# Expert weights' low parts on VectorE, and the float64 decode started with the first expert

## The chip, the cores and the metric

The kernel runs on one core of one Trainium2 chip. The metric is the device time of one execution in microseconds (us); 0.3% of it is about what a measurement of this kernel can tell from no change. The engines are TensorE (PE, with its weight loads as PEld), VectorE (DVE), ScalarE (ACT), GpSimd (POOL) and SyncE (SP, whose queue SPq issues nearly all DMAs). Each engine works its own instructions strictly in the order of its queue.

## What is computed

Three layers in a row on 3072 tokens of 320 numbers (4 sequences of 768, 8 heads of 40):

```
attention:  state = state * w_t - (state @ a_t) b_t + v_t k_t ;  y_t = r_t @ state      (768 steps)
experts:    e = argmax(x @ w_gate);  out = gate * (relu(x @ w1[e]) @ w2[e])              (8 experts, 320 -> 1024 -> 320)
last layer: h = x @ w_in;  g = max(h, 0) + alpha * min(h, 0);  out = g @ w_out           (320 -> 2048 -> 320)
```

`w_in` and `w_out` arrive as float64; everything else is float32.

## The kernel before

**Stages.** The attention runs from the start of the span to about 500 us, the experts from 500 to about 760 us, the last layer from there to the end. The change lies in the expert stage alone.

**One expert.** Tokens have been sorted by expert into the DRAM tensor `xs_d` (room for 448 each). `load_x` brings them in, TensorE transposes them (`tr_ps`, L270), ACT and DVE split them into a rounded part `xthi` (L271, L273) and a rest `xtlo` (L274, L276). For each of eight blocks `f` of 128 hidden units TensorE makes `ph` (8 matmuls of 448 columns, `hidden`), ACT writes `hh` = relu(ph) rounded (L1111), DVE writes its rest `hl` (L1114, two pieces, one of them stored behind `hh`), and one block later TensorE adds that block into the four sums `po` (11 matmuls of 320 columns, `layer2`). So a block's `hh` and `hl` have about one block of TensorE's time to be ready. Sums go out through `ye` (L1172 to L1175) to `ys_d`. The first expert is cut in two: 256 tokens first, the other 192 in a second group; `between(f)` is called in the second group only.

**Preparing weights.** `prep_expert(e + 1, engine)`, called in block 1 of expert e, loads six pieces of float32 weights into `raw` (three buffers, L1047 and L1063); ACT rounds each piece into `we` (L1048, L1064), and the engine that was handed over writes the low part, `raw` minus the rounded part, into `we` as well (L1050, L1052, L1065). A buffer of `raw` comes free when the low part is written. Expert 0 is prepared during the attention, on DVE; experts 1 to 7 are prepared on GpSimd.

**The decode.** `decode` turns `w_in` and `w_out` from float64 into float32 in DRAM: 20 chunks, each a load `r64` (512 KB, L1026; two buffers), three bit operations on DVE (L214, L215, L216 into `dec`), a test on ACT (L1030, L1033) and a store (L1034). The profile prints `r64` as `r`. The decoded weights are read back late, as `raw<-w_in`, for the last layer, and split there on GpSimd (before and after alike).

**Order.** A scheduler with a model of its own time lays down the order of each engine's queue when the program is built. A call such as `decode` only sets where in the program the work enters that model; rows can move by several blocks.

Of the kernel before, what the change touches and what calls it, by code (L numbers as in the profile page):

```python
# [236 lines left out]
def whole(gen):  # L237
    for _ in gen:
        pass
# [749 lines left out]
class Moe:  # L989
# [142 lines left out]
    def run(self, ctx, to_flag):  # L1132
        nc, k, tc = self.nc, self.k, self.tc
        for i in (1, 2):
            self.wp.append(ctx.enter_context(tc.tile_pool(name=f"fm_w{i}", bufs=1, reuse_waits="tile")))
        cp = ctx.enter_context(tc.tile_pool(name="fm_c", bufs=1, reuse_waits="tile"))
        sp = self.sp = ctx.enter_context(tc.tile_pool(name="fm_s", bufs=2, reuse_waits="tile"))
        pg = self.pg = ctx.enter_context(tc.tile_pool(name="fm_pg", bufs=2, space=PSUM, reuse_waits="tile"))
        self.ptr = ctx.enter_context(tc.tile_pool(name="fm_pt", bufs=2, space=PSUM, reuse_waits="tile"))
        pb = ctx.enter_context(tc.tile_pool(name="fm_pb", bufs=1, space=PSUM, reuse_waits="tile"))  # L1140
        pa = ctx.enter_context(tc.tile_pool(name="fm_pa", bufs=1, space=PSUM, reuse_waits="tile"))
        sums = lambda: [p.tile([P, DM], F32, name=f"po{t}") for t, p in enumerate((pa, pa, pb, pb))]
        r6 = ExitStack()
        self.r6 = r6.enter_context(tc.tile_pool(name="fm_r6", bufs=1, reuse_waits="tile"))
        self.small = cp.tile([P, 20], F32, name="small")
        self.n_small = 0
        load = self.load_x(0, EARLY)
        nxt = win = prep = w_in = w_out = None
        for e in range(E):
            w1s, w2s = self.wts[e]  # L1150
            po = sums()
            ye = sp.tile([P, 4, DM], F32, name="ye", tag="orow", bufs=1)
            ys = self.rt.ys_d[e * CAP:(e + 1) * CAP, :]

            def group(xt, t0, t1, x0, tiles, ts=None, between=None):

                ts = ts or range(t0, t1)
                n = min(t1 * P, CAP) - t0 * P
                prev = None
                for f in range(NF1):  # L1160
                    hh, hl = tiles(f)
                    self.hidden(w1s, f, xt, x0, x0 + n, hh, hl)
                    if prev is not None:
                        self.layer2(po, *prev, w2s, f - 1, NF1, True, ts, t0)
                    prev = hh, hl
                    if between:
                        between(f)
                self.layer2(po, *prev, w2s, NF1 - 1, NF1, True, ts, t0)

            def to_sbuf(t):  # L1170
                if t == 3:
                    nc.scalar.copy(ye[:HT, t, :], po[t][HT:])  # L1172
                    nc.vector.tensor_tensor(ye[:HT, t, :], po[t][:HT], ye[:HT, t, :], op=ALU.add)
                else:
                    (nc.vector.tensor_copy if t % 2 else nc.scalar.copy)(ye[:, t, :], po[t])  # L1175

            def between(f):
                nonlocal nxt, win, prep, w_in, w_out
                if e == E - 2 and f == 4:
                    win = self.whole("win")  # L1180
                    prep = self.prep_in(win, w_in, nc.gpsimd)
                if e == E - 2 and f >= 4:
                    for _ in range(2):
                        next(prep, None)
                if e == E - 1:
                    with tc.issue_after(self.hh_i.ins):
                        next(prep, None)
                if f == 1 and e + 1 < E:
                    with tc.issue_after(self.rt.last.ins), tc.issue_after(self.x_dma.ins):
                        whole(self.prep_expert(e + 1, nc.gpsimd))  # L1190
                if (e, f) == (E - 1, 4):
                    assert self.n_small == 20
                    to_flag(self.psum_t(P)[:1], self.small)
                if (e, f) == (1, 0):
                    with tc.issue_after(self.hh_i.ins), tc.issue_after(self.hl_i.ins):
                        w_in, w_out = self.decode(self.w_in, "w_in"), self.decode(self.w_out, "w_out")
                if f == 4 and e + 1 < E:
                    nxt = self.load_x(e + 1)()

            ring = lambda f: [sp.tile([P, 4 * P], F32R, name=n, tag=n) for n in ("hh", "hl")]  # L1200
            if e == 0:
                group(self.xt0, 0, EARLY, 0, lambda f: [self.ap.tile([P, EARLY * P], F32R, name=n, bufs=2) for n in ("ehh", "ehl")])
                xt = load()
                group(xt, EARLY, 4, 0, ring, between=between)
            elif e == E - 1:

                hs = [[hp.tile([P, 2 * P], F32R, name=f"{n}{f}") for n in ("hh", "hl")] for f in range(NF1)]
                group(xt, 0, 2, 0, lambda f: hs[f], (0,), between)
                to_sbuf(0)
                nc.sync.dma_start(ys[:P, :], ye[:, 0])  # L1210
                with tc.issue_after(self.last.ins):
                    for f in range(NF1):
                        self.layer2(po, *hs[f], w2s, f, NF1, True, (1,))
                    group(xt, 2, 4, 2 * P, ring)
            else:
                group(xt, 0, 4, 0, ring, between=between)
            for t in range(1 if e == E - 1 else 0, 4):
                to_sbuf(t)
            for rows, to in self.rows(ye, ys, 1 if e == E - 1 else 0):
                nc.sync.dma_start(to, rows)  # L1220
            if e == E - 2:
                r6.close()
                hp = ctx.enter_context(tc.tile_pool(name="fm_h", bufs=1, reuse_waits="tile"))
                wout = self.whole("wout")
                prep = self.prep_out(wout, w_out, nc.gpsimd)
                win = win.rearrange("p (c f) -> p c f", c=5)
                wout = wout.rearrange("p (s f d) -> p s f d", s=2, d=DM)
            xt = nxt

        al = cp.tile([P, NF2], F32, name="al")  # L1230
        nc.sync.dma_start(al, self.alpha.rearrange("(f p) -> p f", p=P))
        BT = 512
        xt = self.load_x2(0, (E - 1) * CAP + P)
        for i in range(N // BT):
            po = sums()
            prev = None
            for f in range(NF2):
                ph = pg.tile([P, BT], F32, name="ph")
                gemm_k(nc, ph, win, f * P, (f + 1) * P, xt, 0, BT)
                g = sp.tile([P, BT], F32, name="g")  # L1240
                nc.vector.tensor_scalar(g, ph, 0.0, al[:, f:f + 1], op0=ALU.min, op1=ALU.mult)  # L1241
                nc.vector.scalar_tensor_tensor(g, ph, 0.0, g, op0=ALU.max, op1=ALU.add)  # L1242
                hh = sp.tile([P, BT], F32R, name="gh", tag="hh")
                hl = sp.tile([P, BT], F32R, name="gl", tag="hl")
                lo = split(nc, hh, hl, g, nc.gpsimd)
                if prev is not None:
                    self.layer2(po, *prev, wout, f - 1, NF2, False)
                prev = (hh, hl)
                if f == 8 and i + 1 < N // BT:
                    with tc.issue_after(lo.ins):  # L1250
                        nxt = self.load_x2(i + 1, E * CAP)
            ot = sp.tile([P, 4, DM], F32, name="ot", tag="orow", bufs=1)
            for j, (b, t) in enumerate(self.tokens(i)):
                self.layer2(po, *prev, wout, NF2 - 1, NF2, False, (j,))
                gate = self.rt.gate[:, b, t:t + 1]
                if j % 2:
                    nc.vector.tensor_scalar(ot[:, j, :], po[j], gate, None, op0=ALU.mult)
                else:
                    nc.scalar.activation(ot[:, j, :], po[j], AF.Copy, scale=gate)
                if j >= 2:  # L1260
                    at = (b * (S // P) + t - 1) * P
                    nc.sync.dma_start(self.out[at:at + 2 * P, :].rearrange("(t p) d -> p t d", p=P), ot[:, j - 2::2])
            xt = nxt
# [91 lines left out]
```

## Time and profile before

| | us |
|---|---|
| median of 3 runs (lowest, highest) | 1121.48 (1121.19, 1124.84) |
| the profiled execution's own time | 1123.27 |
| its span, first to last instruction | 1121.4 |
| TensorE busy in the span | 1016.5 (91%) |
| DVE busy | 671.7 (60%) |
| ACT busy | 587.3 (52%) |
| GpSimd busy | 546.9 (49%) |
| mean granted TensorE clock | 0.941 |

The span is all but 1.9 us of the profiled execution. Shares are means over stages with different limits; the expert stage is read below in stretches that end where expert 0, 1, 2, 3 and 4 write their last output piece (the end of L1173 at 547.7, 583.6, 612.7, 642.9 and 674.8 us).

### The profile page before, as it was taken

How to read it: one execution, taken by the hardware profiler on the slowest of the kernel's cores; microseconds unless marked ns; L12 is line 12 of the kernel's file. 1: busy time of each engine (PE TensorE's matmuls, PEld its weight loads, DVE VectorE, ACT ScalarE, POOL GpSimd, SP SyncE). 2: the span in 40 equal slices, each digit the busy share in tenths (PEclk: the TensorE clock that was granted, in tenths of full speed). 3: DMA queues.
4: the chain of work that ended last, by engine and by line, in shares of the span. 5: the costliest groups of instructions: out<-in, count | busy, mean ns of one | idle time of the engine just before them, and what ended most of it. 6: DMA issues, size and time to landing. Idle time of an engine off the chain costs nothing.

```text
span 1121.4 us, 24836 instructions
## 1 busy us (share of the span) xinstructions
PE 1016.5 (91%) x9597; PEld 895.2 (80%) x9597; DVE 671.7 (60%) x1451; ACT 587.3 (52%) x1481; POOL 546.9 (49%) x496
## 2 busy tenths in 40 slices
PE   3669899899799999889799989999999999999996
PEld 2558778777677877678698879988888898988996
DVE  8885968968589584543588863334444434444532
ACT  3647887788788886764576644432222222221211
POOL 7755664674656423225555444553434343534332
PEclk8669998999899996999899999999999999999998
DMA  4632322332332122416798954420000000000000
GB/s 120 195 118 59 96 62 77 89 92 78 81 79 69 53 64 64 136 37 201 231 296 271 315 152 144 139 83 15 24 24 24 25 25 24 24 25 24 24 1 27
DMA packets 98081, 103.36 MB, mean 92 GB/s; under 512 B 58404, under 2 KB 78884, under 8 KB 97956
## 3 DMA queue, kind: packets, MB, share of 16 engines
q1 hardware_dynamic: 95652, 93.83, 28.2%
q0 software_dynamic: 2304, 7.87, 2.2%
q8 instruction: 78, 1.28, 0.5%
q14 instruction: 47, 0.39, 0.1%
HBM read 79.39 MB, written 22.28 MB: 91 GB/s over the span
## 4 chain that ended last, share of the span: by engine, by line
PE 52%; DVE 6%; DMA 6%; ACT 4%; issue 2%; SPq 0%; POOL 0%; DVEq 0%; ACTq 0%; POOLq 0%
PE ph L243 22%; PE po L243 20%; DMA raw<-in_moe_w_dram 2%; PE sa L660 2%; PE tr_ps L270 1%; PE pp L620 1%; PE yc L676 1%; DMA r<-in_moe_w_in_dram 1%; DVE dec L215 1%; DMA r<-in_moe_w_out_dram 1%; DVE dec L214 1%; PE rvp L631 1%; PE rp L648 1%; PE xp L243 1%; PE lp L488 1%
## 5 line engine op out<-in xcount | busy, mean ns | idle before, releaser
L234 POOL TENSOR_TENSOR gl<-g,gh 128x512 fp32r<-128x512 f32 x96 | 123.7, 1291 | 214.6 <-ACT gh L233 123.2
L233 ACT ACTIVATE gh<-g 128x512 fp32r<-128x512 f32 x96 | 60.8, 633 | 252.0 <-DVE g L1242 172.0
L1241 DVE TENSOR_SCALAR g<-ph,al 128x512 f32<-128x512 f32 x96 | 72.2, 752 | 160.0 <-POOL gl L234 77.7
L243 PE MATMUL ph<-x2thi,win 128*128 128x512 f32 x480 | 159.5, 397 | 0.0
L243 PE MATMUL po<-wout,gh 128*128 128x320 f32 x768 | 139.0, 309 | 0.0
L243 PEld LDWEIGHTS po<-wout,gh 128*128 128x128 f32 x768 | 122.0, 188 | 5.6
L243 PE MATMUL ph<-x2tlo,win 128*128 128x512 f32 x288 | 114.3, 397 | 0.0
L243 PE MATMUL po<-we,hh 128*128 128x320 f32 x480 | 91.2, 317 | 14.1 <-DVE hh L1114 10.0
L243 PEld LDWEIGHTS ph<-x2thi,win 128*128 128x128 f32 x480 | 88.6, 188 | 14.9
L243 PE MATMUL ph<-xthi,we 128*128 128x448 f32 (+2 forms) x360 | 98.0, 344 | 1.0 <-ACT xthi L273 1.0
L243 PEld LDWEIGHTS po<-we,hh 128*128 128x128 f32 x480 | 74.3, 182 | 18.9 <-DVE hh L1114 10.9
L243 PE MATMUL po<-wout,gl 128*128 128x320 f32 x384 | 82.9, 311 | 0.0
L469 POOL TENSOR_TENSOR abd<-ra,q 40x512 f32<-40x512 f32 x44 | 64.4, 1463 | 25.4 <-PE ap L512 13.0
L243 PE MATMUL ph<-xtlo,we 128*128 128x448 f32 (+2 forms) x216 | 74.1, 344 | 0.3 <-DVE xtlo L276 0.3
L488 PE MATMUL lp<-kb,abd 128*128 128x128 f32 x352 | 58.7, 317 | 15.5 <-POOL abd L469 10.0
L634 POOL TENSOR_SCALAR_AFFINE_SELECT va<-vg 64x512 f32<-64x512 f32 x48 | 33.0, 688 | 77.0 <-ACT vg L633 47.5
L243 PEld LDWEIGHTS ph<-xthi,we 128*128 128x128 f32 x360 | 66.6, 195 | 4.4 <-ACT xthi L273 1.1
L1242 DVE SCALAR_TENSOR_TENSOR g<-ph,g 128x512 f32<-128x512 f32 x96 | 66.3, 691 | 3.1
L1111 ACT ACTIVATE hh<-ph 128x448 fp32r<-128x448 f32 (+2 forms) x72 | 34.2, 477 | 61.5 <-PE ph L243 47.1
L243 PEld LDWEIGHTS po<-wout,gl 128*128 128x128 f32 x384 | 64.0, 188 | 3.0
L488 PEld LDWEIGHTS lp<-kb,abd 128*128 128x128 f32 x352 | 50.9, 222 | 19.3 <-POOL abd L469 11.0
L1050 POOL TENSOR_TENSOR we<-raw,we 128x1024 fp32r<-128x1024 f32 x14 | 34.1, 2452 | 65.3 <-ACT we L1048 63.3
(217 smaller groups left out, 2388.3 us busy)
## 6 DMA issues: line engine op xcount, KB each, us to landing
raw<-in_moe_w_dram SPq DMA_DIRECT2D x16, 512.0 KB
rv<-in_rvP_dram SPq DMA_DIRECT2D x48, 160.0 KB
raw<-in_moe_w_dram SPq DMA_DIRECT2D x16, 480.0 KB
kb<-in_kbP_dram SPq DMA_DIRECT2D x44, 160.0 KB
r<-in_moe_w_in_dram SPq DMA_DIRECT2D x10, 512.0 KB
r<-in_moe_w_out_dram SPq DMA_DIRECT2D x10, 512.0 KB
xs_d<-tt SPq DMA_DIRECT2D x8, 560.0 KB
raw<-in_moe_w_dram SPq DMA_DIRECT2D x16, 256.0 KB
```

The source lines that it names most:

```text
L214: nc.vector.tensor_scalar(t, up, 0x07FFFFFF, 3, op0=ALU.bitwise_and, op1=ALU.logical_shift_left)
L233: nc.scalar.activation(hi, src, AF.Copy)
L234: return lo_eng.tensor_tensor(lo, src, f32(hi), op=ALU.subtract)
L243: return nc.tensor.matmul(out, lhsT=lhsT, rhs=rhs, start=start, stop=stop)
L469: nc.gpsimd.tensor_tensor(abd[r, :, q * C:(q + 1) * C], ra[r], qc[r, :, :C], op=ALU.mult)
L488: nc.tensor.matmul(lp[:, i], lhsT=abd[:, i, c2, :], rhs=kb[:, i, c2, :], start=True, stop=True)
L634: nc.gpsimd.affine_select(x.va[:C].rearrange("p a b c -> p (a b) c")[:, :, D:], x.vg[:C].rearrange("p a b c -> p (a b) c")[:, :, D:], patt ...
L660: nc.tensor.matmul(sa[q * 64:q * 64 + 64, i], lhsT=x.pw[:, i, q * C:(q + 1) * C], rhs=x.vg[:, i, q, :], start=True, stop=True)
L1050: eng.tensor_tensor(wt[:, 3 + c, cs], raw, f32(wt[:, c, cs]), op=ALU.subtract)
L1111: self.hh_i = nc.scalar.activation(hh[:, :n], ph[:, :n], AF.Relu)
L1241: nc.vector.tensor_scalar(g, ph, 0.0, al[:, f:f + 1], op0=ALU.min, op1=ALU.mult)
L1242: nc.vector.scalar_tensor_tensor(g, ph, 0.0, g, op0=ALU.max, op1=ALU.add)
```

## The change

Two calls in `between` differ. The low parts of experts 1 to 7 are handed to DVE, and `decode` is called in block 0 of expert 0's second group instead of block 0 of expert 1.

```diff
                 if f == 1 and e + 1 < E:
                     with tc.issue_after(self.rt.last.ins), tc.issue_after(self.x_dma.ins):
-                        whole(self.prep_expert(e + 1, nc.gpsimd))
+                        whole(self.prep_expert(e + 1, nc.vector))
...
-                if (e, f) == (1, 0):
+                if (e, f) == (0, 0):
                     with tc.issue_after(self.hh_i.ins), tc.issue_after(self.hl_i.ins):
                         w_in, w_out = self.decode(self.w_in, "w_in"), self.decode(self.w_out, "w_out")
```

What stands in the queues changes with it, from expert 0's second group into expert 5; the attention and the last layer keep their order. DVE, expert 0's second group, from block 1 to block 2 (`hh`/`hl` of one block, then of the next). Before:

```order
L1114 SCALAR_TENSOR_TENSOR hh_7297<-ph_7299,hh_7297 128x64
L1114 SCALAR_TENSOR_TENSOR hl_7298<-ph_7299,hh_7297 128x128
L1114 SCALAR_TENSOR_TENSOR hh_7342<-ph_7344,hh_7342 128x64
L1114 SCALAR_TENSOR_TENSOR hl_7343<-ph_7344,hh_7342 128x128
L1114 SCALAR_TENSOR_TENSOR hh_7361<-ph_7363,hh_7361 128x64
```

The same place now (`we1` is expert 1's weights):

```order
L1114 SCALAR_TENSOR_TENSOR hl_7500<-ph_7501,hh_7499 128x128
L215 SCALAR_TENSOR_TENSOR dec_7300<-r64_7298,dec_7300 128x512
L274 TENSOR_TENSOR xtlo_7605<-tr_ps_7606,xthi_7604 128x448
L215 SCALAR_TENSOR_TENSOR dec_7310<-r64_7308,dec_7310 128x512
L274 TENSOR_TENSOR xtlo_7605<-tr_ps_7613,xthi_7604 128x448
L216 SCALAR_TENSOR_TENSOR dec_7300<-r64_7298,dec_7300 128x512
L1065 TENSOR_TENSOR we1_7518<-raw_7532,we1_7518 128x960
L216 SCALAR_TENSOR_TENSOR dec_7310<-r64_7308,dec_7310 128x512
L1065 TENSOR_TENSOR we1_7518<-raw_7536,we1_7518 128x960
L1114 SCALAR_TENSOR_TENSOR hh_7544<-ph_7546,hh_7544 128x64
```

Where two blocks followed each other directly, eight operations now stand between them: four of the decode, two of expert 1's tokens, two low parts.

SP's queue, as expert 1's loads begin. Before:

```order
L1078 DMA xe_7104<-xs_d_79 64x320
L1047 DMA raw_7317<-in_moe_w1_dram 128x1024
L1047 DMA raw_7321<-in_moe_w1_dram 128x1024
L1047 DMA raw_7325<-in_moe_w1_dram 64x1024 x2
L1026 DMA r64_7516<-in_moe2_w_in_dram 128x1024
L1026 DMA r64_7526<-in_moe2_w_in_dram 128x1024
```

Now:

```order
L1078 DMA xe_7104<-xs_d_79 64x320
L1026 DMA r64_7298<-in_moe2_w_in_dram 128x1024
L1026 DMA r64_7308<-in_moe2_w_in_dram 128x1024
L1047 DMA raw_7519<-in_moe_w1_dram 128x1024
L1047 DMA raw_7523<-in_moe_w1_dram 128x1024
L1047 DMA raw_7527<-in_moe_w1_dram 64x1024 x2
```

The first two loads of the decode, which stood behind the first three pieces of expert 1's weights, now stand ahead of them.

DVE at the start of expert 4 (its blocks 0 and 1), before:

```order
L214 TENSOR_SCALAR dec_7699<-r64_7697 128x512
L1114 SCALAR_TENSOR_TENSOR hh_8515<-ph_8517,hh_8515 128x64
L1114 SCALAR_TENSOR_TENSOR hl_8516<-ph_8517,hh_8515 128x384
L215 SCALAR_TENSOR_TENSOR dec_7699<-r64_7697,dec_7699 128x512
L1114 SCALAR_TENSOR_TENSOR hh_8566<-ph_8568,hh_8566 128x64
L1114 SCALAR_TENSOR_TENSOR hl_8567<-ph_8568,hh_8566 128x384
L216 SCALAR_TENSOR_TENSOR dec_7699<-r64_7697,dec_7699 128x512
L214 TENSOR_SCALAR dec_7709<-r64_7707 128x512
L215 SCALAR_TENSOR_TENSOR dec_7709<-r64_7707,dec_7709 128x512
L1114 SCALAR_TENSOR_TENSOR hh_8591<-ph_8593,hh_8591 128x64
```

In the changed program the last decode operation stands ahead of expert 3's last output piece, and expert 4's blocks have only low parts between them.

## Rows read from the trace of the kernel before

**Rows 1.** The page, part 1: busy us (share of the span) x instructions.

```profile
PE 1016.5 (91%) x9597; PEld 895.2 (80%) x9597; DVE 671.7 (60%) x1451; ACT 587.3 (52%) x1481; POOL 546.9 (49%) x496
```

**Rows 2.** Stretches by expert: us, busy us of each engine, granted clock, DMA share, GB/s.

```profile
517.80:547.70 29.90, 27.08 (x171) 24.01 (x169) 11.55 (x32) 17.61 (x34) 19.69 (x10) 0.94 0.68 213
547.70:583.60 35.90, 31.27 (x172) 28.51 (x170) 28.98 (x43) 24.13 (x47) 20.22 (x9) 0.90 0.84 277
583.60:612.70 29.10, 27.10 (x154) 24.31 (x153) 23.30 (x39) 17.73 (x33) 13.64 (x6) 1.00 0.83 282
612.70:642.90 30.20, 29.71 (x173) 27.03 (x172) 26.55 (x41) 21.06 (x40) 14.26 (x6) 1.00 0.94 313
642.90:674.80 31.90, 27.36 (x149) 24.74 (x149) 21.28 (x31) 15.20 (x28) 14.48 (x6) 0.95 0.56 174
```

**Rows 3.** TensorE in time: start, us, operation [idle before it, who ended it].

```profile
553.96 0.63 PE L243 MATMUL po<-we,hh 128*128 128x320 f32 x1 [4.63 <-DVE hh L1114]
...
656.82 0.41 PE L243 MATMUL po<-we,hh 128*128 128x320 f32 x1 [3.55 <-DVE hh L1114]
```

**Rows 4.** DVE in time, ahead of the first of these waits.

```profile
547.60 2.95 DVE L215 SCALAR_TENSOR_TENSOR dec<-r,dec 128x512 uint32<-128x512 uint32 x2
550.48 3.30 DVE L216 SCALAR_TENSOR_TENSOR dec<-r,dec 128x512 uint32<-128x512 uint32 x2
```

**Rows 5.** The tile dec: DVE operations, ns min/median/max, first and last start.

```profile
L214 DVE TENSOR_SCALAR dec<-r x20: 409/426/2620, 545.2 to 651.6; 128x512 uint32<-128x512 uint32 x20
L215 DVE SCALAR_TENSOR_TENSOR dec<-r,dec x20: 675/693/2772, 547.6 to 654.1; 128x512 uint32<-128x512 uint32 x20
L216 DVE SCALAR_TENSOR_TENSOR dec<-r,dec x20: 673/692/2695, 550.5 to 657.2; 128x512 uint32<-128x512 uint32 x20
```

**Rows 6.** The stretches of rows 2 for tile dec alone: DVE busy, clock, DMA.

```profile
517.80:547.70 29.90, 2.17 (x3) 0.94 0.68 213
547.70:583.60 35.90, 20.09 (x19) 0.90 0.84 277
583.60:612.70 29.10, 15.83 (x16) 1.00 0.83 282
612.70:642.90 30.20, 19.01 (x18) 1.00 0.94 313
642.90:674.80 31.90, 12.86 (x7) 0.95 0.56 174
```

**Rows 7.** Groups by line, GpSimd, 517.8 to 674.8: busy us, mean ns, idle before.

```profile
L1050 POOL TENSOR_TENSOR we<-raw,we 128x1024 fp32r<-128x1024 f32 x12 | 29.3, 2458 | 48.3 <-ACT we L1048 46.3 <-PE po L243 2.0
```

**Rows 8.** DVE in time during the attention: low parts of expert 0's weights.

```profile
451.29 1.23 DVE L1050 TENSOR_TENSOR we<-raw,we 128x1024 fp32r<-128x1024 f32 x1 [4.83 <-DMA raw<-in_moe_w_dram]
...
459.65 1.16 DVE L1065 TENSOR_TENSOR we<-raw,we 128x960 fp32r<-128x960 f32 x1
...
462.00 0.83 DVE L1065 TENSOR_TENSOR we<-raw,we 128x640 fp32r<-128x640 f32 x1
```

**Rows 9.** Who waited for whom, 517.8 to 674.8: us in total, times, longest.

```profile
ACT we L1048 <- DMA raw<-in_moe_w_dram: 7.5, 7, 3.4
DVE dec L214 <- DMA r<-in_moe_w_in_dram: 5.6, 4, 3.0
ACT we L1064 <- DMA raw<-in_moe_w_dram: 3.4, 4, 1.4
DVE dec L214 <- DMA r<-in_moe_w_out_dram: 3.3, 3, 1.8
```

**Rows 10.** ACT in time: expert 1's second and third weight piece.

```profile
517.71 1.06 ACT L1048 ACTIVATE we<-raw 128x1024 fp32r<-128x1024 f32 x1 [0.49 <-DMA raw<-in_moe_w_dram]
...
520.18 1.06 ACT L1048 ACTIVATE we<-raw 128x1024 fp32r<-128x1024 f32 x1 [1.14 <-DMA raw<-in_moe_w_dram]
```

**Rows 11.** SP's queue in time: the decode's last store, the read-back's first load.

```profile
658.62 0.34 SPq L1034 DMA_DIRECT2D w_out<-dec  x1
...
684.65 4.85 SPq L1047 DMA_DIRECT2D raw<-w_in  x4
```

## The prediction

> **What bounds the kernel now.** I read the page's first part, then TensorE's waits in the expert stage, then what the engine they name was doing. TensorE is busy 91% of the span [rows 1], so a gain can only come out of its pauses and of stretches at half clock. The change touches experts 0 to 4 most, and the stretches [rows 2] give what is to be had there: a stretch's length minus TensorE's busy time is 2.8, 4.6, 2.0, 0.5 and 4.5 us for experts 0 to 4. The granted clock adds to it: 0.94, 0.90 and 0.95 in the stretches of experts 0, 1 and 4 are 1.8, 3.6 and 1.6 us of full clock not granted; of the 3.6 I count 2.4, since part of it falls into the pause itself.
>
> The two long pauses have one cause. TensorE stands 4.63 us at 553.96 and 3.55 us at 656.82, both times until DVE has written a block's rest into `hh` [rows 3]. Ahead of the first, DVE's queue holds two decode operations of L215 for 2.95 us and two of L216 for 3.30 us [rows 4]. The same operations take 0.68 us when undisturbed; single ones go up to 2.77, and L214 goes from 0.41 to 2.62 [rows 5]. What lengthens them is about as long as one low part on GpSimd (2.46 us on average, [rows 7]). In the time of experts 0 to 4 the decode costs DVE 70.0 us, the sum of [rows 6]; 20 chunks at 0.43 + 0.69 + 0.69 = 1.81 us, the medians of [rows 5], would be 36.2. So some 34 us of DVE are spent standing behind GpSimd.
>
> **The change, part by part.** (1) *The low parts leave GpSimd.* Forty-two operations of about 2.46 us go [rows 7]; no decode operation meets GpSimd work any more, so I put the decode at 1.81 us a chunk. GpSimd does not wait for anything afterwards that matters: its next work is the read-back's split, unchanged.
>
> (2) *They arrive on DVE.* The same operations ran on DVE for expert 0: 1.23 us for a piece of 1024 columns, 1.16 for 960, 0.83 for 640 [rows 8]. An expert costs 3 x 1.23 + 2 x 1.16 + 0.83 = 6.8 us of DVE. A buffer of `raw` comes free earlier by about 1.2 us than behind GpSimd where DVE is on time.
>
> (3) *The decode starts an expert earlier.* Its end buys nothing by itself: the last store is issued at 658.62 and the first read-back at 684.65 [rows 11], 26 us apart. What it does is spread the 20 chunks over experts 0 to 3, by the new order 4.7, 5, 5.3 and 5 of them, and free expert 4. It also puts two loads of 512 KB ahead of expert 1's weights on SP's queue; two neighbouring pieces of that size reach ACT 2.5 us apart [rows 10]. Behind them wait ACT, DVE and with them the blocks of expert 0's second group, whose weights are long there.
>
> Now the load of DVE. Its other work is what [rows 2] holds beyond [rows 6]: 9.4, 8.9, 7.5, 7.5 and 8.4 us. To that come the low parts and chunks that the new order puts into each stretch:
> - expert 0: 9.4 + nine low parts 10.5 + decode 8.4 = 28.3 us in a stretch of 29.9
> - expert 1: 8.9 + nine low parts 10.0 + decode 9.1 = 28.0; TensorE's own floor is 35.9 - 4.6 - 2.4 = 28.9
> - expert 2: 7.5 + 6.8 + 9.7 = 24.0 against 27.1; expert 3: 7.5 + 6.8 + 9.1 = 23.4 against 29.7
> - expert 4: 8.4 + 6.8 = 15.2 against 31.9 - 4.5 - 1.6 = 25.8.
>
> In experts 2 to 4 DVE has room, and its longest single operation falls from 2.77 us to 1.23, so their pauses should go: 2.0 + 0.5 + 6.1 = 8.6 us. In expert 1 it just fits: 7.0 us at best. In expert 0 there is no room: I count no gain. Together 15.6 us before new waits.
>
> (4) *New waits.* DVE now stands in its queue for weight pieces, through ACT, and for chunks, with `hh` and `hl` of the next block behind it; TensorE waits for those. The trace does not show that, so I bound it. From below: no wait that TensorE feels, 0. From above: in experts 0 and 1 every one of about ten chunks waits one transfer of 2.5 us [rows 10], 25 us. Between them I take the waits that the trace has for the same loads [rows 9]. L214 waited 5.6 + 3.3 = 8.9 us for 20 chunks; half the chunks now fall where DVE has no room, 4.5 us. ACT waited 7.5 + 3.4 = 10.9 us for six experts' weights, of which two and a half are prepared there, 4.5 us; as both loads share one queue, half of that is the same wait, 2.3 us. Pauses of TensorE in expert 0 and 1 cost clock as before; I leave 2.0 us for it, near the 1.8 of expert 0 now. Sum 8.8 us, nearer to the lower end because the trace's own waits for these loads lie there.
>
> A rule that speaks against the change: with DVE saturated, the Trainium skill (Perfetto Trace Analysis, section Optimizing Scalar/DVE Operations) says that offloading to ScalarE or even GpSimd may make sense; this goes the other way. The same place warns that the two share a port, so that moving work between them might not help; the stretched decode operations of [rows 4] agree with that warning. By the rule alone DVE's queue would be the new bound, which is the slower rival below.
>
> **The sum.** 15.6 - 8.8 = 6.8 us. The profiled execution took 1123.27 us, its span 1121.4, and the median of the runs is 1121.48, so I take the gain off the median: about 1115 us. Experts 5 to 7 I leave as they are: they get 6.8 us of low parts each and no decode, and expert 4's 15.2 us of DVE show the room there. The last layer's order is unchanged.
>
> **The rivals.**
> - *The new waits hardly show.* The first two chunks are loaded far ahead, and a faster release of `raw` brings the weights earlier. For it: the DMA engines stand at 0.68 in expert 0's stretch [rows 2]. Against: expert 0's stretch now takes 4.7 chunks, where only three decode operations ran in it [rows 6], and their loads and stores come through the same queue. With waits of 0 to 4.4 us the time is 1106 to 1110.
> - *A wash.* DVE becomes the bound in experts 0 and 1 and stalls there eat what experts 1 to 4 give back. For it: 28.3 of 29.9 us and 28.0 of 28.9 leave it 2.5 us of slack in 65. Against: GpSimd's 2.46 us blocks are gone. With waits of 12 to 19 us the time lies within 0.3% of before, 1118 to 1125; its middle is 1121. That the decode's new place does nothing (above) belongs here: it would then only bring the chunks into the fullest stretch.
> - *Slower.* SP's queue and DVE's hold each other up in experts 0 and 1: each new load of a chunk stands behind the store of the chunk two before it, the store behind DVE, DVE behind a weight piece that SP has not issued yet. If each of ten chunks pays 2.5 us [rows 10] and the clock halves for it over 2 us more, 27 us are lost against 15.6: 1133. It ends slower as soon as the waits in these two stretches pass 19 us, about two thirds of that. For it: eight operations stand between two neighbouring blocks of expert 0 where none stood. Against: the same bytes went through the same queue at a share of 0.84 to 0.94 in experts 1 to 3 [rows 2] with 8.9 us of such waits in all.
>
> **How the numbers follow.** About 0.3% (3.4 us) is what a measurement of this kernel can tell from no change. My forecast, a gain of 3.4 to 11 us, gets 0.44; hardly any waits 0.16; a wash 0.23; slower 0.17. So faster 0.60, same 0.23, slower 0.17. The time is 1115. The range reaches from 1107, waits of about 1 us, to 1126, waits of about 20 us; that leaves some 0.05 below and 0.15 above.
>
> **What would show it.** Right: the decode's operations at 0.41 to 0.70 us throughout and no pause of TensorE above 2 us that a DVE rest ends after expert 1; the decode over before expert 3's output; expert 4's stretch near 26 to 28 us; DVE above 90% busy in expert 0's stretch, with that stretch no shorter than now. Wrong: expert 0's or expert 1's stretch longer by more than 5 us, with TensorE waiting for `hh` and DVE for `raw` or `r`; or the low parts on DVE longer than 1.3 us; or pauses of experts 2 to 4 still there with DVE idle, which would mean that ACT or the loads, and not GpSimd, had set them.

## The result and the profile after

The changed kernel takes 1112.52 us, the median of 6 runs (1110.4 to 1116.11), against 1122.8 us for the kernel before beside it (1119.82 to 1125.29, 6 runs): a ratio of 0.9912, 95% interval 0.9885 to 0.9939, or 10.3 us. In two later comparisons it came to 0.9946 (0.9917 to 0.9975) and 0.9922 (0.9892 to 0.9952), 7.1 and 7.7 us. It is faster, by 0.5 to 0.9% in the three comparisons. The forecast was 6.8 us.

The profiled execution after took 1111.37 us, its span 1109.6. Part 1 of its page of the profile, against [rows 1]:

```profile
PE 1012.1 (91%) x9597; PEld 894.1 (81%) x9597; DVE 682.5 (62%) x1493; ACT 586.2 (53%) x1481; POOL 447.0 (40%) x454
```

GpSimd gave up 100 us and DVE took on only 11, because the decode became cheaper on it. The tile `dec` after, against [rows 5] (ns min/median/max, first and last start), and the groups of low parts on DVE, against [rows 7] (busy us, mean ns, idle before):

```profile
L214 DVE TENSOR_SCALAR dec<-r x20: 405/424/430, 526.1 to 630.2; 128x512 uint32<-128x512 uint32 x20
L215 DVE SCALAR_TENSOR_TENSOR dec<-r,dec x20: 671/683/695, 527.1 to 631.1; 128x512 uint32<-128x512 uint32 x20
L216 DVE SCALAR_TENSOR_TENSOR dec<-r,dec x20: 670/683/694, 529.4 to 631.8; 128x512 uint32<-128x512 uint32 x20
```

```profile
L1065 DVE TENSOR_TENSOR we<-raw,we 128x960 fp32r<-128x960 f32 (+1 forms) x21 | 21.5, 1040 | 4.8 <-ACT we L1064 4.8
L1050 DVE TENSOR_TENSOR we<-raw,we 128x1024 fp32r<-128x1024 f32 x14 | 16.9, 1221 | 3.3 <-ACT we L1048 3.2
L1052 DVE TENSOR_TENSOR we<-raw,we 64x1024 fp32r<-64x1024 f32 x7 | 8.6, 1222 | 2.2 <-ACT we L1048 2.1
```

No operation of the decode is lengthened any more: the longest takes 0.695 us, where it was 2.772. The low parts cost what they cost for expert 0 in [rows 8].

The stretches after, against [rows 2], cut at the start of each expert's last output piece (L1173). Expert 0's begins here with its first matmul, since the attention ends 2.2 us later in this execution with the same order; the first fence is before cut in that way.

```profile
500.42:547.20 46.78, 43.09 (x281) 39.52 (x282) 17.36 (x60) 21.63 (x43) 22.35 (x12) 0.93 0.58 178
```

```profile
502.62:552.19 49.57, 44.19 (x280) 40.49 (x281) 33.42 (x83) 27.48 (x59) 1.96 (x2) 0.90 0.75 239
552.19:580.06 27.87, 27.87 (x167) 26.16 (x166) 25.52 (x48) 21.61 (x40) 0.00 (x0) 1.00 0.98 325
580.06:607.65 27.59, 26.46 (x158) 24.79 (x157) 23.42 (x45) 17.99 (x36) 0.00 (x0) 1.00 0.96 309
607.65:634.92 27.27, 26.89 (x160) 24.97 (x160) 23.13 (x46) 19.57 (x37) 0.00 (x0) 1.00 0.86 289
634.92:662.67 27.75, 27.75 (x165) 25.90 (x164) 15.19 (x28) 12.46 (x22) 0.00 (x0) 1.00 0.51 153
```

Experts 1 to 4 now run at a granted clock of 1.00 (2.4 GHz all through) and TensorE is busy for nearly all of each stretch. Cut alike, before's stretches were 46.8, 35.9, 29.1, 30.2 and 31.9 us. So expert 0 lost 2.8 us, and experts 1 to 4 gave 8.1, 1.5, 2.9 and 4.2: 13.9 us in this pair of executions, of which the span shows 11.8, since the attention ended 2.2 us later.

All pauses of TensorE above 0.6 us in experts 0 to 4, against [rows 3]:

```profile
524.75 0.56 PE L243 MATMUL po<-we,hh 128*128 128x320 f32 x2 [1.81 <-ACT hh L1111]
...
533.60 0.89 PE L270 MATMUL tr_ps<-ident,xe 128*128 128x128 f32 x4 [2.55 <-DMA xe<-xs_d]
...
584.06 0.33 PE L270 MATMUL tr_ps<-ident,xe 64*128 64x64 f32 x2 [1.13 <-DMA xe<-xs_d]
```

None is ended by a rest of DVE. The first is a wait in ACT's queue: a weight piece waits 0.93 us for its load there and takes 1.06, and `hh` stands behind it (ACT in time):

```profile
523.42 1.06 ACT L1048 ACTIVATE we<-raw 128x1024 fp32r<-128x1024 f32 x1 [0.93 <-DMA raw<-in_moe_w_dram]
524.38 0.31 ACT L1111 ACTIVATE hh<-ph 128x192 fp32r<-128x192 f32 x1
```

### The profile page after: what moved, and what is told of

Same layout as the page of the kernel before. It is cut to its first block, busy times and chain, and to the rows that moved or that the text cites. A ratio compares the mean times of both kernels' runs of the same rounds, so it can differ in the third digit from the quotient of the medians.

```text
span 1109.6 us, 24830 instructions
## 1 busy us (share of the span) xinstructions
PE 1012.1 (91%) x9597; PEld 894.1 (81%) x9597; DVE 682.5 (62%) x1493; ACT 586.2 (53%) x1481; POOL 447.0 (40%) x454
## 4 chain that ended last, share of the span: by engine, by line
PE 55%; DMA 5%; DVE 5%; ACT 3%; issue 2%; POOL 0%; SPq 0%; DVEq 0%; ACTq 0%; POOLq 0%
PE ph L243 23%; PE po L243 22%; DMA raw<-in_moe_w_dram 2%; PE sa L660 2%; DMA xe<-xs_d 2%; PE tr_ps L270 2%; PE pp L620 1%; PE yc L676 1%; PE rvp L631 1%; PE rp L648 1%; PE xp L243 1%; PE lp L488 1%; ACT bds L691 1%; PE yp L585 1%; POOL wout L1065 0%
## 5 line engine op out<-in xcount | busy, mean ns | idle before, releaser
L243 PE MATMUL po<-we,hh 128*128 128x320 f32 (+1 forms) x480 | 90.1, 317 | 3.6 <-ACT hh L1111 3.6
L1050 POOL TENSOR_TENSOR win<-raw,win 128x1024 fp32r<-128x1024 f32 x4 | 9.6, 2409 | 181.2 <-ACT win L1048 181.1
L243 PEld LDWEIGHTS po<-we,hh 128*128 128x128 f32 (+1 forms) x480 | 74.2, 183 | 6.9 <-ACT hh L1111 4.1
L660 PE MATMUL sa<-vg,pw 128*64 128x104 f32 x768 | 58.9, 269 | 7.5 <-ACT vg L650 7.2
L546 DVE TENSOR_TENSOR ut<-ut,tmp 128x31 f32<-128x31 f32 (+15 forms) x186 | 62.4, 336 | 3.7
```

The costliest lines, as they stand in the source:

```text
L243: return nc.tensor.matmul(out, lhsT=lhsT, rhs=rhs, start=start, stop=stop)
L546: nc.vector.tensor_tensor(ut[:, j + 1:, :m], ut[:, j + 1:, :m], tv, op=ALU.subtract)
L660: nc.tensor.matmul(sa[q * 64:q * 64 + 64, i], lhsT=x.pw[:, i, q * C:(q + 1) * C], rhs=x.vg[:, i, q, :], start=True, stop=True)
```

## The experiments

All were timed beside the kernel before on their own chip, four kernels to a chip; ratios are to that, with 95% intervals.

### Each half alone, both, and more low parts on DVE

Only the low parts (low_only) and only the decode's start (decode_only):

```diff
-                        whole(self.prep_expert(e + 1, nc.gpsimd))
+                        whole(self.prep_expert(e + 1, nc.vector))
```

```diff
-                if (e, f) == (1, 0):
+                if (e, f) == (0, 0):
```

> Only the low parts of experts 1 to 7 move to DVE; the decode stays with expert 1. Theory A (the gain is the end of the waiting of the decode's DVE operations behind GpSimd): nearly all of the gain is here, 8 to 12 us below before; the decode's operations stay at 0.40 to 0.70 us; no pause of TensorE above 2 us ended by a DVE rest. Theory B (the gain comes from spreading the decode over one more expert and freeing expert 4): at most 3 us below before. Expert 0's second group should be as short as before or shorter, since no decode stands in it.

> Only the decode moves to expert 0; the low parts stay on GpSimd. Theory A: no gain, within 4 us of before or slower, with the decode's operations still up to 2.5 us and longer waits in expert 0's second group, where GpSimd now works on expert 1's weights at the same time. Theory B: 6 us or more below before.

The whole change once more, and the whole change with the low parts of the last layer's `wout` on DVE as well:

> The changed kernel once more, on the same chip as its two halves: 8 to 12 us below before. If theory A holds it differs from low_only by less than 4 us, and from the cost of expert 0's stretch (longer by 2.8 us in the first profile) it would be the slower of the two; if the two halves work together only, it is more than 4 us faster than low_only.

```diff
-                prep = self.prep_out(wout, w_out, nc.gpsimd)
+                prep = self.prep_out(wout, w_out, nc.vector)
```

> The changed kernel, and the low parts of w_out for the last layer on DVE as well. The chain of waits runs through these GpSimd operations between expert 7 and the last layer, where TensorE stands for 1.3 and 0.4 us. If they set the start of the last layer: 1 to 3 us below the changed kernel. If the gather of tokens on GpSimd's queue waits for the last expert's output anyway: the same within 1 us.

Measured, before at 1122.5: low_only 1114.76 (0.9939, 0.9909 to 0.997), decode_only 1112.47 (0.9919, 0.989 to 0.9948), both_again 1115.36 (0.9946, 0.9917 to 0.9975), wout_dve 1118.92 (0.9961, 0.9933 to 0.9989). The intervals of the first three overlap: **either half gives about the whole gain, and the two don't add.** Neither of my two theories had that; low_only and both_again, 7.7 and 7.1 us below before, also came out a little under the 8 to 12 expected. It can be so if both halves take away the same pauses by different means, and the stretches bear that out. Those of experts 1 and 4, which held the two long pauses and took 35.9 and 31.9 us, with only the low parts moved (busy us of each engine as in [rows 2]):

```profile
542.29:572.94 30.65, 28.54 (x166) 26.26 (x165) 25.21 (x48) 19.92 (x39) 0.00 (x0) 1.00 0.98 320
635.64:663.15 27.51, 27.44 (x161) 25.13 (x160) 16.82 (x34) 13.38 (x25) 0.00 (x0) 1.00 0.55 163
```

and with only the decode's start moved:

```profile
547.71:578.73 31.02, 31.02 (x183) 28.55 (x182) 27.48 (x44) 23.73 (x46) 18.48 (x9) 1.00 0.95 304
638.75:665.38 26.63, 26.63 (x159) 24.78 (x158) 8.69 (x22) 11.54 (x20) 12.20 (x6) 1.00 0.65 185
```

In decode_only the lengthened operations are still there:

```profile
L214 DVE TENSOR_SCALAR dec<-r x20: 410/456/2570, 524.2 to 631.3; 128x512 uint32<-128x512 uint32 x20
L215 DVE SCALAR_TENSOR_TENSOR dec<-r,dec x20: 676/693/2700, 529.4 to 632.1; 128x512 uint32<-128x512 uint32 x20
L216 DVE SCALAR_TENSOR_TENSOR dec<-r,dec x20: 676/693/2522, 532.4 to 635.4; 128x512 uint32<-128x512 uint32 x20
```

but the longest pause that a rest ends is this one (TensorE and DVE in time), where [rows 3] has 4.63 and 3.55:

```profile
529.37 0.41 PE L243 MATMUL po<-we,hh 128*128 128x320 f32 x1 [2.45 <-DVE hh L1114]
```

```profile
524.24 4.93 DVE L214 TENSOR_SCALAR dec<-r 128x512 uint32<-128x512 uint32 x2
529.10 0.21 DVE L1114 SCALAR_TENSOR_TENSOR hh<-ph,hh 128x64 fp32r<-128x64 f32 x1
```

wout_dve gained nothing over both_again, where 1 to 3 us or no change was expected: its median is 3.6 us higher, though the two intervals overlap. TensorE there waits three times 0.63 to 0.69 us for `hl` between 720 and 729 us.

### Where the decode starts, and how much DVE bears

From this a third theory: a pause needs several decode operations between two rests in DVE's queue (a bunch, which the scheduler's order makes) and GpSimd busy beside them, which lengthens each. The kernel before has two such bunches. The first is the four operations of [rows 4] and, ahead of them, two of L214 (2.07 + 2.95 + 3.30 = 8.3 us); the second, ahead of the wait at 656.82, is three operations of 7.3 us together (DVE in time):

```profile
545.21 2.07 DVE L214 TENSOR_SCALAR dec<-r 128x512 uint32<-128x512 uint32 x2
...
649.34 2.29 DVE L216 SCALAR_TENSOR_TENSOR dec<-r,dec 128x512 uint32<-128x512 uint32 x1
651.55 2.47 DVE L214 TENSOR_SCALAR dec<-r 128x512 uint32<-128x512 uint32 x1
654.06 2.58 DVE L215 SCALAR_TENSOR_TENSOR dec<-r,dec 128x512 uint32<-128x512 uint32 x1
```

The kernel before with other starts, its low parts on GpSimd:

```diff
-                if (e, f) == (1, 0):
+                if (e, f) == (2, 0):
```

> The kernel before with the decode asked for one expert later, at (2, 0), the low parts still on GpSimd. Each half of the change alone gave about the whole gain, so two theories are left. Spreading: the gain of the earlier decode comes from its being spread over more stretches; then 20 stretched chunks squeezed into experts 2 to 4 are denser than before, and the time is 1122 or more, up to 1130. Bunching: what cost the time was only that the scheduler set two chunks back to back (six stretched operations) between two rests of a block at expert 1's start, and three more chunks near expert 4's start; with the start moved either way those two places change, and the later start gives a gain as well, 1110 to 1118.

```diff
-                if (e, f) == (1, 0):
+                if (e, f) == (0, 6):
```

> The kernel before with the decode asked for two blocks earlier only, at (0, 6). Spreading: the chunks lie in nearly the same stretches as before, so the time is within 3 us of before, 1119 to 1125. Bunching: the two chunks that stood between two rests are now split over two blocks of expert 0's end, where TensorE's queue is different, so most of the 4.63 us pause and its clock go: 1112 to 1118.

The kernel before with a third of the decode's DVE work:

```diff
-            f64_bits(nc, dec, r64)
+            nc.vector.tensor_scalar(dec.bitcast(U32), r64[..., 1], 0x07FFFFFF, 3, op0=ALU.bitwise_and, op1=ALU.logical_shift_left)
```

> The kernel before with the decode's second and third operation (L215, L216) left out, so the weights that it stores are not the reference's; the low parts stay on GpSimd and the decode starts at (1, 0). If the stretched operations of the decode in DVE's queue made the two long pauses, they go although GpSimd works as before: the time is 1108 to 1116 and no pause above 2 us is ended by DVE in experts 1 to 4. If the pauses came from GpSimd's own lateness with the weights (raw freed late, we late) or from the loads, they stay: 1119 or more.

low_only with each low part written twice; the same loop stands around the other two lines that write low parts. The pieces of L1052 are written over their own operand, so the second time puts the rounded weights back there and leaves out those low parts; the time is that of the doubled work.

```diff
-                    eng.tensor_tensor(wt[:, 3 + c, cs], raw, f32(wt[:, c, cs]), op=ALU.subtract)
+                    for _ in range(times):
+                        eng.tensor_tensor(wt[:, 3 + c, cs], raw, f32(wt[:, c, cs]), op=ALU.subtract)
...
-        yield from self.prep_in(wt[:, :self.HW], self.w1[e], eng)
-        yield from self.prep_out(wt[:, self.HW:], self.w2[e], eng)
+        yield from self.prep_in(wt[:, :self.HW], self.w1[e], eng, 2 if e else 1)
+        yield from self.prep_out(wt[:, self.HW:], self.w2[e], eng, 2 if e else 1)
```

> The kernel with the low parts on DVE and the decode at (1, 0), with each low part of experts 1 to 7 computed twice on DVE, 6.8 us more of DVE work for an expert. If DVE's load as a sum is what counts (its slack in experts 1 to 4 was worked out as 0 to 5 us), it costs 10 to 25 us against the single one, 1122 to 1140. If only long blocks between two rests count, the short 1.2 us operations fit between, and it costs 0 to 4 us: up to 1119.

Measured, before at 1120.11: dec_2_0 1119.76 (1.0014, 0.9987 to 1.0041), dec_0_6 1118.06 (0.9982, 0.9952 to 1.0012), one_bit_pool 1104.91 (0.9885, 0.9846 to 0.9925), low_twice 1129.01 (1.0085, 1.0059 to 1.0112).

- **one_bit_pool** went below the range expected, with no pause above 0.5 us ended by DVE in experts 0 to 4: the decode's operations made the pauses, not late weights or loads, since GpSimd did the same work as before and still lengthened the operation that was left (its tile `dec`, ns min/median/max). How much of its gain is the shorter sums and how much the saved DVE time, it does not tell.

```profile
L1029 DVE TENSOR_SCALAR dec<-r x20: 407/698/2614, 542.3 to 627.2; 128x512 uint32<-128x512 uint32 x20
```

- **dec_2_0 and dec_0_6** gained nothing, which went against my guess that any other start breaks the bunches; both medians lie between the ranges of the two theories, dec_0_6 within 0.1 us of the upper end of bunching. The bunches only move: dec_2_0 has pauses of 4.49 and 4.24 us, dec_0_6 one of 4.19. DVE ahead of dec_2_0's first, three lengthened operations in a row:

```profile
601.34 0.41 DVE L214 TENSOR_SCALAR dec<-r 128x512 uint32<-128x512 uint32 x1
601.79 2.76 DVE L215 SCALAR_TENSOR_TENSOR dec<-r,dec 128x512 uint32<-128x512 uint32 x1
604.58 2.75 DVE L216 SCALAR_TENSOR_TENSOR dec<-r,dec 128x512 uint32<-128x512 uint32 x1
607.25 2.56 DVE L214 TENSOR_SCALAR dec<-r 128x512 uint32<-128x512 uint32 x1
609.73 0.21 DVE L1114 SCALAR_TENSOR_TENSOR hh<-ph,hh 128x64 fp32r<-128x64 f32 x1
```

- **low_twice** has no lengthened decode (0.694 us at most) and no pause above 1.7 us, and still lies 0.0146 of 1120 us, 16 us, above low_only by their ratios: many small pauses, and expert 0's stretch at 54.3 us against 44.1 in low_only. So DVE's load does count. In the profiles experts 1 to 4 together took only 2.7 us more than in low_only, so the load cost most in expert 0's stretch. Whether the room that the prediction worked out (0.9 to 6.3 us a stretch, 10.6 in expert 4) is right, this run does not show, since its decode lies in other stretches.

### Bunches or place

Starts (0, 0), (0, 6), (1, 0) and (2, 0) also stand in order of time, so "an earlier place is better" explained the times as well. Two kernels to tell these apart: an early start whose order has a bunch of six, and a late one with the low parts on DVE.

```diff
-                if (e, f) == (1, 0):
+                if (e, f) == (0, 3):
```

> The kernel before with the decode asked for at (0, 3), the low parts still on GpSimd. Against the start at (0, 0) it stays in the same stretches, experts 0 to 3, but the order of DVE puts six decode operations between two rests at once (none but two gaps of four at (0, 0)), and six gaps hold four or more. Theory of the earlier place: it is as fast as the start at (0, 0), 8 to 10 us below the kernel before, 1110 to 1114. Theory of the bunches (a gap between two rests that holds several operations lengthened by GpSimd makes a pause): at least one pause of 3 us or more that a DVE rest ends, behind a gap of 7 us or more of decode, and 0 to 4 us below the kernel before, 1116 to 1123.

```diff
-                        whole(self.prep_expert(e + 1, nc.gpsimd))
+                        whole(self.prep_expert(e + 1, nc.vector))
...
-                if (e, f) == (1, 0):
+                if (e, f) == (2, 0):
```

> The low parts on DVE and the decode asked for one expert later than before, at (2, 0): the same late place that gave nothing with the low parts on GpSimd, and by the order nine gaps of four decode operations or more. Theory of the bunches: without GpSimd beside them six operations last 3.6 us and four 2.4, no gap of decode reaches 4.5 us and no rest makes a pause above 2 us: 1110 to 1117. Theory of the place: a late decode is slow whichever engine has the low parts, 1119 or more.

And an attempt to take the pauses for `xe` out of the changed kernel, with the changed kernel beside it:

```diff
-            self.x_dma = self.nc.sync.dma_start(to, rows)
+            self.x_dma = (self.nc.gpsimd if e else self.nc.sync).dma_start(to, rows)
```

> The changed kernel with the loads of the tokens of experts 1 to 7 (xe) issued by GpSimd, which has nothing else to do there, instead of SP's queue, where they stand behind weight pieces that wait for a free buffer. TensorE's pauses for xe in the changed kernel are 2.55 + 1.13 + 0.38 us. If the place in SP's queue makes them, they go: 2 to 5 us below the changed kernel of the same chip. If the transfer itself is late (DMA engines full) or GpSimd issues it slowly, they stay: within 2 us of it.

> The changed kernel beside the three others on one chip, as the measure for them: 5 to 10 us below the kernel before.

Measured, before at 1117.14: dec_0_3 1108.84 (0.9912, 0.9879 to 0.9944), low_2_0 1108.5 (0.9922, 0.9894 to 0.995), xe_pool 1113.65 (0.9962, 0.9936 to 0.9989), after_third 1109.44 (0.9922, 0.9892 to 0.9952).

**low_2_0** settles the place by itself: the late start that gave nothing beside GpSimd gives the whole gain without it (the median is 1.5 us below the range that the bunches gave). Its longest decode operations and its longest pause ended by DVE:

```profile
L215 DVE SCALAR_TENSOR_TENSOR dec<-r,dec x20: 672/685/693, 564.4 to 654.0; 128x512 uint32<-128x512 uint32 x20
```

```profile
604.11 0.56 PE L243 MATMUL po<-we,hh 128*128 128x320 f32 x2 [1.22 <-DVE hh L1114]
```

**dec_0_3** is split. The bunch of six did what it was said to do, in expert 0 (DVE, then TensorE, which waits through `xtlo` behind the same bunch):

```profile
526.61 4.11 DVE L214 TENSOR_SCALAR dec<-r 128x512 uint32<-128x512 uint32 x2
530.65 4.80 DVE L215 SCALAR_TENSOR_TENSOR dec<-r,dec 128x512 uint32<-128x512 uint32 x2
535.37 1.28 DVE L216 SCALAR_TENSOR_TENSOR dec<-r,dec 128x512 uint32<-128x512 uint32 x2
```

```profile
537.24 1.09 PE L270 MATMUL tr_ps<-ident,xe 128*64 128x128 f32 x4 [6.47 <-DVE xtlo L274]
```

but the time went below what the bunches allowed, and 8.3 us below before it is what the theory of the earlier place had (8 to 10). From the traces, one execution each: the longest sums of decode operations between two neighbouring rests in DVE's queue (waits for loads not counted), the longest pause that a result of DVE ends in experts 0 to 4, and the time from expert 0's first matmul to expert 4's last output piece:

| kernel | low parts | start | longest decode between rests, us | longest pause by DVE, us | experts 0 to 4, us | ratio |
|---|---|---|---|---|---|---|
| before | GpSimd | (1, 0) | 8.3, 7.3 | 4.63, 3.55 | 173.9 | 1 |
| dec_2_0 | GpSimd | (2, 0) | 8.5, 7.7 | 4.49, 4.24 | 171.5 | 1.0014 |
| dec_0_6 | GpSimd | (0, 6) | 9.5 | 4.19 | 169.6 | 0.9982 |
| dec_0_3 | GpSimd | (0, 3) | 10.2 | 6.47 | 165.7 | 0.9912 |
| decode_only | GpSimd | (0, 0) | 5.1 | 2.45 | 162.3 | 0.9919 |
| low_only | DVE | (1, 0) | 2.9 | 1.38 | 165.0 | 0.9939 |
| low_2_0 | DVE | (2, 0) | 3.5 | 1.22 | 161.5 | 0.9922 |
| changed | DVE | (0, 0) | 2.7 | 0.53 | 160.1, 162.0, 166.2 | 0.9912, 0.9946, 0.9922 |

Each sum above 7 us has a pause of 3.5 us or more behind it, and none up to 5.7 us has one above 2.5 (in dec_2_0's second, 2.6 us of waiting for a load come on top). With one such bunch or none experts 0 to 4 are faster than with two, in this column of profiles. The medians do not follow the bunches as closely: dec_0_6 with one gains nothing, and dec_0_3, with a pause of 6.47 us in its profile, has a median as low as those without. Its profiled execution, 1112.68 us, is the slowest of its eight, so the pause may be shorter in most; one profile for an order can't tell.

So it is not shown why an early start gains beside GpSimd. A rival that no run sets apart: decode_only and dec_0_3 leave expert 4 all but free of decode (0 and 1 of its operations start in that stretch, of 26.6 and 27.2 us), while dec_0_6, the kernel before and dec_2_0 have 5, 7 and 19 there, in 35.2, 31.9 and 34.8 us. With the low parts on GpSimd the two early starts gain and the three later ones do not; with the low parts on DVE the place makes no difference that the intervals show, and low_2_0, with 18 of the decode's operations starting in expert 4, has that stretch at 29.4 us.

**xe_pool** came out 4.2 us above the changed kernel beside it, outside both ranges, and was wrong in its reason. The order has TensorE transpose the next tokens right after the ones before, from the one buffer of `xe`; the load can start only when those are read, whichever queue issues it. SP issued it at 529.89 in the changed kernel and TensorE went on at 533.60. GpSimd issued it no earlier (31.5 us after expert 0's first matmul against 27.3), and TensorE went on 8.3 us behind it (GpSimd and TensorE in time):

```profile
528.66 1.30 POOL L1078 DMA_DIRECT2D xe<-xs_d  x2 [12.56 <-PE tr_ps L270]
```

```profile
536.93 0.87 PE L270 MATMUL tr_ps<-ident,xe 128*128 128x128 f32 x3 [6.31 <-DMA xe<-xs_d]
```

The later two pauses for `xe` did go, but the first cost more. Of the versions that do the whole work none is faster than the changed kernel by more than the measurement is uncertain.

## Why the prediction was right, and where it was not

- **The cause of the long pauses held.** That DVE's rests came late behind lengthened decode operations, and that these were lengthened by GpSimd's low parts, was read from [rows 4, 5, 7]. In the trace of before all 21 lengthened operations (over 1.3 times their median) overlap a low part on GpSimd, and none of the 32 that meet none is lengthened. low_only and low_2_0 (no such operation, no long pause) and one_bit_pool (fewer operations beside the same GpSimd work, no pause by DVE) bear it out. One reading was too wide: 2.46 us in [rows 7] is the piece of 1024 columns, and all 42 low parts took 97.4 us, 2.32 us each; no term of the sum hangs on it.
- **The terms of experts 1 to 4 held.** 8.6 us were worked out for experts 2 to 4 and 1.5 + 2.9 + 4.2 = 8.6 came, though expert 3 gave more and expert 4 less than its own figure; 7.0 for expert 1 and 8.1 came. That the sum was met to the tenth is luck: in the two other profiles of the changed kernel experts 2 to 4 gave 8.4 and 5.8 us and expert 1 8.4 and 7.0. The price of the low parts (1.2 us) and of a chunk (1.8 us) was met. Expert 4 has 27.8 us, within the 26 to 28 named, and the decode ends ahead of expert 3's output.
- **The term of new waits was mis-sized.** 8.8 us were set for experts 0 and 1. Expert 1 had none above 0.6 us; expert 0's stretch grew by 2.8 us here and by 4.9 and 5.0 in the other two profiles. In this one TensorE stood 5.4 us in it instead of 3.7, and was busy 44.2 us instead of 43.1 at a granted clock of 0.90 instead of 0.93. The loads' own waits in experts 0 and 1 were near what was assumed, 3.2 us on L214 and 2.4 on ACT (4.5 and 4.4, 5.2 and 3.9 in the other two) against 4.5 and 4.5, but in this profile only one above 0.6 us reached TensorE, through ACT. In their place stood one that the prediction did not have: for `xe`, 2.6 us in expert 0 and 4.1 in experts 0 to 4 (these waits in experts 0 to 4 are below, against [rows 9]). By the profiles the forecast came out 7.1 us short in this pair (13.9 against 6.8), by the medians 3.5, and by the two later comparisons 0.3 and 0.9.

```profile
ACT we L1064 <- DMA raw<-in_moe_w_dram: 4.4, 4, 1.5
ACT we L1048 <- DMA raw<-in_moe_w_dram: 4.3, 4, 1.9
PE tr_ps L270 <- DMA xe<-xs_d: 4.1, 3, 2.6
DVE dec L214 <- DMA r<-in_moe_w_in_dram: 3.2, 2, 2.5
DVE dec L214 <- DMA r<-in_moe_w_out_dram: 2.2, 4, 1.0
```

- **Part (3) was priced too low.** The sum has no gain for the decode's start without the low parts: the spread and the free expert 4 are counted only together with the shorter operations, and "the decode's new place does nothing" stands under a wash. decode_only gave as much as the whole. The prediction looked at the length of single operations; that several stood between two rests, [rows 4] had shown (two and two, 6.25 us), and the new order could have been read for that. Which of its effects gives the start its gain stays open, as said above.
- **DVE's busy share in expert 0** was to pass 90%; in the last 29.9 us of that stretch it is 0.83 (24.96 us). That the stretch does not get shorter was right. The rivals by which DVE becomes the bound, or DVE's queue and SP's hold each other up, did not come about; low_twice shows that the first can: 6.8 us more of DVE for each expert make it slower than before.

## What to carry to other kernels

When a pause of the busiest engine is ended by a short operation, add up all that stands in that queue since the last such operation, and not only the longest piece: here sums above 7 us had pauses of 3.5 us or more behind them and smaller ones had not, and a sum falls either if each piece gets shorter or if fewer stand there. Two halves of a change that remove the same pause are worth it once, so time each alone before adding them up. And read a new order for the rows between two neighbours on the path, since another start asked for in the program (here (0, 3), (0, 6) and (2, 0)) can move the bunches without removing them.

## What was not expected of the hardware

Side by side, DVE paid and GpSimd hardly did. In decode_only the second of two operations of L214 in the row at 524.24 above ended at 529.17, behind the third of these low parts (GpSimd in time), which ended at 528.89:

```profile
521.68 4.72 POOL L1050 TENSOR_TENSOR we<-raw,we 128x1024 fp32r<-128x1024 f32 x2 [10.51 <-ACT we L1048]
526.48 2.41 POOL L1052 TENSOR_TENSOR we<-raw,we 64x1024 fp32r<-64x1024 f32 x1
```

Where decode operations went from 0.41 to 2.57 and from 0.68 to 2.70 us, the low parts of 1024 columns on GpSimd kept in the median the time of the same operations on the last layer's weights, which ran after the decode was over (ns min/median/max):

```profile
L1050 POOL TENSOR_TENSOR we<-raw,we x14: 2365/2396/2950, 521.7 to 668.4; 128x1024 fp32r<-128x1024 f32 x14
L1050 POOL TENSOR_TENSOR win<-raw,win x4: 2399/2410/2417, 694.2 to 704.4; 128x1024 fp32r<-128x1024 f32 x4
```

The longest is 0.55 us above the median, about one undisturbed decode operation. The Trainium skill (SBUF — State Buffer, section Who interferes with whom) says, of a DVE instruction in a mode that uses both of its ports, that whoever issues first gets the port pair shared with GpSimd for the whole instruction while the other blocks. In which mode the decode's operations ran no row shows, but the lengths agree with such a hold: the longest of each line lies 1.8 to 2.2 us above its shortest, less than one low part (2.40), and the longest low part 0.55 us above its median, less than one decode operation of L215 or L216 (0.68). The same low part took 1.22 us on DVE against 2.40 on GpSimd.

In xe_pool a load of `xe` issued by GpSimd took 3.7 to 8.1 us from issue to landing (median 5.2).
